# Issuing 18 of 24 output stores from GpSimd's queue in place of SyncE's

## The chip, the cores and the metric

The kernel runs on one core of one Trainium2 chip. The metric is the device time of one execution in microseconds; a kernel is given by the median of its runs. The engines are named as the profile names them: PE is TensorE (PEld its weight loads), DVE is VectorE, ACT is ScalarE, POOL is GpSimd, SP is SyncE. "SPq" and "POOLq" are the instruction streams of SyncE and GpSimd where they issue DMAs or wait.

## The reference

Inputs r, k, v, w, a, b have the shape (4 batches, 8 heads, 768 steps, 40), all float32. A recurrence runs over the steps; its output, laid out as 3072 tokens of 320, goes through a feed-forward block with a squared ReLU and 2048 hidden units. The output is float32, 3072 x 320.

```python
for t in range(S):
    y[:, :, t] = einsum('bhd,bhde->bhe', rt, state)
    Sa = einsum('bhde,bhe->bhd', state, at)
    state = state * wt[:, :, None, :] - einsum('bhd,bhe->bhde', Sa, bt) + einsum('bhd,bhe->bhde', vt, kt)
x = y.transpose(0, 2, 1, 3).reshape(3072, 320)
h = maximum(x @ w_in, 0.0)
out = (h * h) @ w_out
```

## The kernel before, in words

The 768 steps are cut into 6 chunks of 128. One chunk of one batch is a "load group" m (24 of them): six input tiles of 160 KB (NW, NK, NB, NA, NV, NR) are loaded for each by SyncE (`add_load`, line 272), into rings of four buffers per input. They are turned into the operands of the recurrence: ScalarE takes a logarithm of w (lnW, line 286) and exponentials (GI, GA); GpSimd or VectorE splits lnW in two differences (r at line 304, lo at line 308), multiplies k and b by GI (KB, line 331), and casts a, r and v (GA, RV, EVX, line 234). The operands are then transposed. For the later groups SyncE does that by a transposing DMA (line 374): KBT from KB, RVT from RV, A from GA. These DMAs stand in the same queue as the loads, and each waits until its source tile is written. For the earlier groups TensorE transposes through PSUM (line 346).

Each group has two "steps" of two head pairs, in which TensorE and VectorE work out the chunk's result within itself and with the state carried from the chunk before (matmuls at lines 477 to 590, products at lines 485, 571, 595). The result is YS. It leaves the head layout by four small DMAs on SyncE per feed-forward block (line 712, YS<-YS).

The feed-forward block (`add_ff`) runs over 14 sets of tokens (`FFS`): the groups 0 to 3 singly and then ten pairs. Each set makes hidden tiles: a product with WIN in a PSUM bank (line 723), a ReLU to hs on ScalarE or VectorE (line 731 or 733; a ring of three buffers), and a square to Gt on GpSimd, VectorE or ScalarE (line 742 or 740). For each group of the set the product of Gt with WOUT (line 760) is gathered in one bank, copied by ScalarE or VectorE to a tile osb of 128 x 320 float32 (a ring of three buffers) and stored to the output by one DMA of 160 KB (`store`, line 768). There are 24 such stores. The weights WIN and WOUT are loaded once, between 15 and 58 us, by DMAs that GpSimd issues (lines 680 and 688) and that cast to bfloat16 on the way.

The order in which the operations are emitted is written out by hand (`ORDER`), together with the choice of the engine for those that may run on more than one (`WAYS`). Each engine carries out its own instructions in the order in which they were emitted, so a store stands in its issuer's stream at the place that `ORDER` gives it, and what stands behind it on that engine waits for it. An osb buffer is written again only when the store of its former content has landed, by a semaphore. `add_guard` sums up energies of intermediate values; its verdict (`bad`, line 822) is read by all engines near the end and starts a general path if the fast one isn't accurate enough; with these inputs it is not taken.

TensorE's instructions are by name: line 477 `ca` (reads KBT and A's product AT), line 566 `ex` (reads RVT), line 509 corrections, line 582 `kbm`, line 590 `z`.

Of the kernel before, what the change touches and what calls it, by code (L numbers as in the profile page):

```python
# [18 lines left out]
def kernel(  # L19
# [12 lines left out]
    nc = tc.nc  # L32

    NB, NHH, T, D = r.shape
    L = 128
# [44 lines left out]
    def buf(ring, kind=None):  # L80
        b_ = Buf(ring, kind)
        if ring != "bank":
            row = rings.setdefault(ring, [])
            b_.n = len(row)
            row.append(b_)
        return b_

    def op(name, eng, rank, cost, lat, needs, bufs, fn, mode=None, alts=()):

        o = Op()  # L90
        o.name, o.eng, o.rank, o.cost, o.lat, o.mode = name, eng, rank, cost, lat, mode
        o.alts = [(eng, cost, lat), *alts] if alts else []
        o.needs, o.bufs, o.end, o.order = list(needs), list(bufs), None, len(ops)
        o.fn = (lambda: fn(o.eng)) if alts else fn
        o.dma = o.idle = None
        for b_ in o.bufs:
            b_.users.append(o)
        assert name not in ops, name
        ops[name] = o
# [21 lines left out]
    def act(n, more=0.0):  # L121
        return 0.093 + 0.00083 * n + more, 0.186 + 0.00083 * n

    def pe(n):
        return n, n + 0.165

    def vec(n, each=0.00104):
        return 0.065 + each * n, 0.148 + each * n
# [21 lines left out]
    for ring, shape in (("KB", [128, 2, NHH, 64]), ("GA", [128, 2, NHH, 64]),  # L150
# [9 lines left out]
        out=UTI[:], in_=ones_f[:], pattern=[[1, 128]],  # L160
# [5 lines left out]
        out=IDb[:], in_=ones_b[:], pattern=[[1, 128]],  # L166
# [3 lines left out]
    for s in range(2):  # L170
        nc.gpsimd.tensor_copy(out=IDs[64 * s:64 * s + D, :],
                              in_=IDb[64 * s:64 * s + D, 64 * s:64 * s + D])
    for i in range(26):
# [3 lines left out]
        out=UTb[:], in_=ones_b[:], pattern=[[1, 128]],  # L177
# [4 lines left out]
        out=MEX[:], in_=MEX[:], pattern=[[0, 4], [1, L]],  # L182
# [46 lines left out]
    def copy(eng, out, in_, scale=None):  # L229
        if eng == "ACT":  # L230
            nc.scalar.activation(out=out, in_=in_, func=ACTF.Copy,  # L231
                                 **({} if scale is None else {"scale": scale}))
        elif scale is None:
            (nc.gpsimd if eng == "POOL" else nc.vector).tensor_copy(out=out, in_=in_)
        else:
            nc.vector.tensor_scalar(out=out, in0=in_, scalar1=scale, scalar2=None, op0=ALU.mult)  # L236
# [22 lines left out]
    def sb(b_, shape, dtype):  # L259
        if b_.tile is None:  # L260
            pool = natp if b_.ring[0] == "N" else rot
            b_.tile = pool.tile(shape, dtype, name=b_.ring, tag=b_.ring,
                                bufs=RING[b_.ring if b_.ring in RING else "N"])
        return b_.tile
# [430 lines left out]
    FFS = [(0,), (1,), (2,), (3,)] + [(m, m + 1) for m in range(4, NBC, 2)]  # L695
    Gtb = [buf("Gt") for _ in FFS]

    def add_ff(h):
# [56 lines left out]
        for b_ in range(nb):  # L755
            opb, osbb = buf("bank", "ff"), buf("osb")

            def ff_out(part_, b_=b_, opb=opb):
                for j in range(part_ * NJ // 2, (part_ + 1) * NJ // 2):
                    nc.tensor.matmul(out=opb.tile[:, 0:DM], lhsT=Gtb[h].tile[:, j, b_, :],  # L760
                                     rhs=WOUT[:, j, :], start=(j == 0), stop=(j == NJ - 1))

            def copy_out(eng, opb=opb, osbb=osbb):
                copy(eng, sb(osbb, [128, DM], FP32)[:], opb.tile[:, 0:DM])

            def store(b_=b_, osbb=osbb):
                tok = (b0 + b_) * T + c * L
                nc.sync.dma_start(out=out[tok:tok + L, :], in_=osbb.tile[:])

            k = NJ // NU // 2  # L770
            for p in range(2):
                op(("op", h, b_, p), "PE", last + 12.8 + 1.8 * b_ + 0.3 * p, *pe(1.085),
                   [("Gt", h, k * p + i) for i in range(k)] + [("WOUT", 2 * p), ("WOUT", 2 * p + 1)]
                   + ([("op", h, b_, 0)] if p else []),
                   [Gtb[h], opb], lambda p=p, f=ff_out: f(p), "F")
            op(("osb", h, b_), "ACT", last + 13.5 + 1.8 * b_, *act(302), [("op", h, b_, 1)],
               [opb, osbb], copy_out, alts=[("DVE", *vec(320))])
            op(("st", h, b_), "SP", last + 1.6 + 1.8 * b_, 0.45, 0.45, [("osb", h, b_)], [osbb], store)
            ops["st", h, b_].dma = "h", 0.5
# [309 lines left out]
```

## Time and profile before

| | us |
|---|---|
| median of 3 runs | 272.27 |
| lowest and highest | 271.66 and 272.66 |
| the profiled execution | 272.03 |
| its span, first to last instruction | 270.3 |

The profiled execution ran at a mean granted TensorE clock of 0.981; the clock is below full only in the first quarter. DMA engines moved 37.61 MB, 34.33 MB of them through the queue of SyncE (75.6% of 16 engines' span) and 2.62 MB through that of GpSimd (6.6%).

How to read it: a row of a timeline has the start in us from the span's start, the duration in us, the engine, the source line, the operation, what it writes and reads, and how many were merged; in square brackets the idle time of the engine before it and what ended it. A row of the list of waits has who waited for whom, the total in us, the number of waits and the longest. A row of the stretches has, for each engine, its busy time and its instructions, and then the granted clock, the DMA engines' share and GB/s. A row of the DMA issues ends with the median time from issue to landing, in us. Matmuls are pipelined and overlap in the timeline, so TensorE's starts tell more than its durations.

### The profile page before, as it was taken

The page shows a single profiled execution, that of the slowest core. Times are in us where ns is not written, and L with a number is a line of the kernel's source. Part 1 is how long each engine was busy: PE and PEld are TensorE (multiplying, and loading weights), DVE is VectorE, ACT ScalarE, POOL GpSimd, SP SyncE. Part 2 cuts the span into 40 slices and gives each one's busy share as a digit, 9 for nine tenths or more (in the row PEclk, how much of TensorE's full clock was granted, in tenths as well). Part 3 has the DMA queues.
Part 4 walks back from the last instruction along what each step waited for, and adds up shares of the span by engine and source line. Part 5 has one row for each costly group of instructions (what it writes and reads, how often), then busy time and mean ns, then how long its engine had stood idle before and what let it go on. Part 6 is the DMA issues. An engine that isn't in the chain of part 4 may idle for free.

```text
span 270.3 us, 10143 instructions
## 1 busy us (share of the span) xinstructions
PE 254.8 (94%) x3944; PEld 205.7 (76%) x3944; DVE 241.0 (89%) x564; ACT 206.8 (77%) x542; POOL 186.2 (69%) x313
## 2 busy tenths in 40 slices
PE   7885989799999999999999999999999999999994
PEld 6653668578888778778888778888888777778773
DVE  7785899999999999999999999999999888898382
ACT  3474778888999979888999878787888767966560
POOL 4396947896979797799978668786945574143360
PEclk9998589999999999999999999999999999999999
DMA  7999999997983995898897889998999978904002
GB/s 120 172 179 158 155 168 174 166 183 124 158 150 59 184 150 94 157 182 145 162 175 143 149 156 150 184 140 160 165 124 118 180 130 166 153 11 112 6 29 75
DMA packets 184034, 37.61 MB, mean 139 GB/s; under 512 B 178544, under 2 KB 183664, under 8 KB 183984
## 3 DMA queue, kind: packets, MB, share of 16 engines
q1 hardware_dynamic: 181328, 34.33, 75.6%
q0 software_dynamic: 2656, 2.62, 6.6%
q8 instruction: 31, 0.51, 0.8%
q14 instruction: 19, 0.16, 0.2%
HBM read 28.84 MB, written 3.93 MB: 121 GB/s over the span
## 4 chain that ended last, share of the span: by engine, by line
PE 62%; DVE 14%; DMA 6%; SPq 5%; ACT 4%; issue 4%; POOL 3%; DVEq 0%; POOLq 0%; ACTq 0%
PE bank L723 19%; PE bank L760 14%; PE bank L346 5%; SPq L272 5%; PE bank L582 5%; PE bank L477 4%; DVE CN L485 4%; PE bank L509 3%; PE bank L566 3%; DVE EVX L571 3%; PE bank L300 2%; PE bank L590 2%; DMA KBT<-KB 2%; DVE YS L595 2%; DMA NA<-in_a_dram 2%
## 5 line engine op out<-in xcount | busy, mean ns | idle before, releaser
L723 PE MATMUL bank<-YS,WIN 120*128 120x256 bf16 (+3 forms) x672 | 75.0, 257 | 0.3 <-DVE CN L485 0.3
L571 DVE TENSOR_TENSOR EVX<-bank,MEX 128x512 bf16<-128x512 f32 x96 | 63.8, 679 | 2.2 <-PE bank L566 1.7
L485 DVE TENSOR_TENSOR CN<-bank,MCN 128x512 bf16<-128x512 f32 x96 | 62.8, 679 | 2.0 <-PE bank L477 1.3
L723 PEld LDWEIGHTS <-WIN 120*128 120x128 bf16 (+1 forms) x672 | 54.6, 97 | 7.6 <-issue 0.4
L760 PE MATMUL bank<-WOUT,Gt 128*128 128x320 bf16 x384 | 58.6, 299 | 0.0
L742 POOL TENSOR_TENSOR Gt<-hs 128x512 bf16<-128x512 bf16 x38 | 39.6, 1044 | 26.6 <-ACT hs L731 14.5
L731 ACT ACTIVATE hs<-bank 128x512 bf16<-128x512 f32 x74 | 42.9, 596 | 8.2 <-PE bank L723 3.2
L760 PEld LDWEIGHTS <-Gt 128*128 128x128 bf16 x384 | 34.9, 97 | 12.4 <-issue 0.2
L534 ACT ACTIVATE junk<-CN 128x512 bf16<-128x512 bf16 x48 | 30.1, 628 | 1.5 <-DVE CN L485 1.0
L526 POOL TENSOR_TENSOR x<-Mc,c 128x160 f32<-128x160 bf16 x41 | 20.8, 510 | 13.5 <-DVE c L522 11.8
L331 POOL TENSOR_TENSOR KB<-NB,GI 128x320 bf16<-128x320 f32 (+1 forms) x22 | 18.8, 856 | 12.7 <-DMA NB<-in_b_dram 12.6
L530 POOL TENSOR_TENSOR Cc<-x,EVX 128x160 bf16<-128x160 f32 x46 | 23.3, 513 | 2.9 <-DVE EVX L236 1.4
L509 PEld LDWEIGHTS <-CN 128*128 128x128 bf16 x384 | 19.6, 97 | 5.8 <-issue 1.8
L582 PE MATMUL bank<-EVX,KB 128*64 128x168 bf16 x384 | 23.4, 245 | 0.1
L331 POOL TENSOR_TENSOR KB<-NK,GI 128x320 bf16<-128x320 f32 (+1 forms) x23 | 19.7, 858 | 5.1 <-ACT GI L321 2.7
L740 ACT ACTIVATE Gt<-hs 128x512 bf16<-128x512 bf16 x35 | 21.7, 632 | 1.2 <-DVE hs L733 1.0
L231 ACT ACTIVATE TB<-bank 128x512 bf16<-128x512 bf16 (+1 forms) x29 | 16.8, 578 | 7.2 <-PE bank L552 4.4
L477 PE MATMUL bank<-AT,KBT 64*128 64x128 bf16 x384 | 19.8, 222 | 2.1 <-ACT KBT L231 1.2
L595 DVE TENSOR_TENSOR YS<-bank,GT 128x256 bf16<-128x256 f32 x48 | 19.6, 413 | 1.3 <-PE bank L582 0.8
L733 DVE TENSOR_SCALAR hs<-bank 128x512 bf16<-128x512 f32 x22 | 14.8, 684 | 5.9 <-issue 3.9
L599 DVE TENSOR_TENSOR UZ<-bank,GT 64x80 bf16<-64x80 f32 x80 | 18.5, 234 | 1.5 <-PE bank L590 0.5
L522 DVE TENSOR_TENSOR c<-bank,Mc 128x160 bf16<-128x160 f32 x48 | 14.9, 314 | 5.4 <-PE bank L509 5.0
(113 smaller groups left out, 587.6 us busy)
## 6 DMA issues: line engine op xcount, KB each, us to landing
NW<-in_w_dram SPq DMA_DIRECT2D x24, 160.0 KB
NB<-in_b_dram SPq DMA_DIRECT2D x24, 160.0 KB
NK<-in_k_dram SPq DMA_DIRECT2D x24, 160.0 KB
NA<-in_a_dram SPq DMA_DIRECT2D x24, 160.0 KB
NV<-in_v_dram SPq DMA_DIRECT2D x24, 160.0 KB
NR<-in_r_dram SPq DMA_DIRECT2D x24, 160.0 KB
out_dram<-osb SPq DMA_DIRECT2D x24, 160.0 KB
WOUT<-in_moe_w_out_dram POOLq DMA_DIRECT2D x4, 320.0 KB, 5.6
```

The costliest lines, as they stand in the source:

```text
L331: engine(eng).tensor_tensor(out=o.KB.tile[:, u, h, 0:D], in0=o.nat[key].tile[:, h], in1=o.GI.tile[:, h], op=ALU.mult)
L477: nc.tensor.matmul(out=quads(ca[s])[:, i, u, :], lhsT=o.KBT.tile[half(s), u, j0 + i, :], rhs=o.AT.tile[half(s), j0 + i, :], start=(i == 0 ...
L485: nc.vector.tensor_tensor(out=t_[:, :, s], in0=quads(ca[s]), in1=MCN[:], op=ALU.mult)
L509: nc.tensor.matmul(out=P[:, 2 * i + s], lhsT=CN[:, i, s, 1, :], rhs=X[:, 2 * i + s], start=False, stop=last, skip_group_check=True)
L534: nc.scalar.activation(out=t_, in_=CN_.tile[:, :, :, 1, :], func=ACTF.Square, accum_out=ACC[:, AN + st:AN + st + 1])
L571: nc.vector.tensor_tensor(out=EVX[:, :, s, 0:2 * LV].rearrange("p i (u x) -> p i u x", u=2)[:, :, :, 0:L], in0=quads(ex[s]), op=ALU.mult, ...
L582: nc.tensor.matmul(out=uy()[half(s), i, :], lhsT=o.KB.tile[:, u, 2 * (j0 + i) + s, :], rhs=EVX[:, i, s, LV * u:LV * u + LV], start=(i == 0 ...
L595: nc.vector.tensor_tensor(out=t_[:, p2, :], in0=uy()[:, :, 0:L], in1=o.GT.tile[:, j0:j0 + 2, 0:L], op=ALU.mult)
L723: nc.tensor.matmul(out=hp[:, u], lhsT=WIN[g][0:ROWS[g], j * 128:(j + 1) * 128], rhs=by_pair()[0:ROWS[g], g], start=(g == 0 and u == 0), st ...
L731: nc.scalar.activation(out=t_, in_=hpb.tile[:], func=ACTF.Relu)
L742: engine(eng).tensor_tensor(out=t_, in0=x_, in1=x_, op=ALU.mult)
L760: nc.tensor.matmul(out=opb.tile[:, 0:DM], lhsT=Gtb[h].tile[:, j, b_, :], rhs=WOUT[:, j, :], start=(j == 0), stop=(j == NJ - 1))
```

## The change

The stores of the sets 4 to 12 of 14 (`h` counts the sets), that is 18 of 24, are issued by GpSimd; those of the first four sets and of the last one stay with SyncE. A DMA issued by GpSimd goes through the other DMA queue. Every operation keeps its place in `ORDER`; in GpSimd's stream a store comes to stand between the operations that were emitted before and after it. The copies to osb, the buffers and the semaphore waits for data and buffers are the same.

```diff
             def store(b_=b_, osbb=osbb):
                 tok = (b0 + b_) * T + c * L
-                nc.sync.dma_start(out=out[tok:tok + L, :], in_=osbb.tile[:])
+                queue = nc.gpsimd if 4 <= h < len(FFS) - 1 else nc.sync
+                queue.dma_start(out=out[tok:tok + L, :], in_=osbb.tile[:])
```

## The prediction

> **What bounds the kernel now.** I read the engines' busy time first, then the same by stage, the chain that ended last, and TensorE's own two waits on it, because all 18 moved stores lie between 127 and 263 us.
>
> ```profile
> PE 254.8 (94%) x3944; PEld 205.7 (76%) x3944; DVE 241.0 (89%) x564; ACT 206.8 (77%) x542; POOL 186.2 (69%) x313
> ```
> ```profile
> core 0: us, PE busy (x) PEld busy (x) DVE busy (x) ACT busy (x) POOL busy (x), PEclk, DMA share, GB/s
> 127.00:200.00 73.00, 72.85 (x1160) 60.07 (x1159) 70.28 (x165) 62.46 (x176) 56.47 (x89) 1.00 0.97 156
> 200.00:235.00 35.00, 34.16 (x513) 27.42 (x512) 30.08 (x68) 27.21 (x68) 18.59 (x30) 1.00 0.87 146
> 235.00:262.00 27.00, 27.00 (x333) 21.87 (x331) 19.68 (x41) 17.16 (x40) 11.68 (x16) 1.00 0.21 51
> ```
> TensorE at full clock is the bound in every stretch that the change touches: of these 135 us it is idle 0.15 + 0.84 + 0 = 0.99 us. GpSimd is busy 56.47 + 18.59 + 11.68 = 86.74 us and idle 48.3. After 127 us SyncE, DMA and GpSimd stand in the chain in one stretch, 209 to 234 us:
>
> ```profile
> 209.18 3.60 DMA NB<-in_b_dram
> 212.92 0.85 POOL KB L331
> ...
> 214.45 1.01 POOL Gt L742
> 215.48 0.61 ACT hs L731
> ...
> 223.13 0.85 SPq L712
> 224.03 2.82 DMA NV<-in_v_dram
> ...
> 227.90 0.86 POOL KB L331
> 228.79 5.11 DMA KBT<-KB
> ```
> A load is issued by SyncE, lands, GpSimd works on it, and the next engine starts 0.02 to 0.03 us after GpSimd ends (214.45 + 1.01 to 215.48; 227.90 + 0.86 to 228.79). Here alone a microsecond of SyncE or of GpSimd reaches TensorE. It waits twice:
>
> ```profile
> 215.73 0.23 PE L477 MATMUL bank<-AT,KBT 64*128 64x128 bf16 x1
> 216.13 0.38 PE L477 MATMUL bank<-AT,KBT 64*128 64x128 bf16 x7 [0.17 <-ACT hs L731]
> ```
> ```profile
> 233.19 0.26 PE L509 MATMUL bank<-c,CN 128*128 128x40 bf16 x4
> 233.94 0.40 PE L477 MATMUL bank<-AT,KBT 64*128 64x128 bf16 x8 [0.50 <-DMA KBT<-KB]
> ```
> By starts, which do not hang on modelled ends, the first wait is 216.13 - 215.73 = 0.40 us less one matmul of under 0.05 (eight of this line take 0.40 with their latency), about 0.35. The second is 0.75 us less four matmuls of about 0.025, some 0.65.
>
> **The price of one moved store.** SyncE loses 18 issues; GpSimd gains 18. The output bytes, the copies into osb and the order on TensorE, VectorE and ScalarE stay.
>
> ```profile
> L768 SPq DMA_DIRECT2D out_dram<-osb x24: 333/524/881, 88.5 to 267.2; - x24
> ```
> ```profile
> 32.73 1.09 POOL L680 DMA_DIRECT2D WIN<-in_moe_w_in_dram  x2
> 40.88 0.81 POOL L688 DMA_DIRECT2D WOUT<-in_moe_w_out_dram  x1
> ```
> SyncE: 18 x 0.524 = 9.4 us of issue time go. GpSimd has issued no store yet; the nearest rows are a WIN load of 40 rows at 1.09 / 2 = 0.55 us and a WOUT load of 128 x 4 rows at 0.81. A store has 128 rows, so I take 0.55 + 0.26 x 88 / 472 = 0.60 us and keep 0.55 and 0.81 as ends. 18 x 0.60 = 10.8 us (9.9 to 14.6) fit four times into GpSimd's 48.3 idle us, so what counts is the place of each.
>
> **Where the new issues stand.** Numbered 1 to 24 in the order of SyncE, stores 5 to 22 move. In the built program each osb copy stands far enough ahead; the nearest is store 17, behind the x at 232.46:
>
> ```profile
> 230.25 0.43 ACT L231 ACTIVATE osb<-bank 128x320 f32<-128x320 f32 x1
> ```
> ```profile
> 232.46 0.60 POOL L526 TENSOR_TENSOR x<-Mc,c 128x160 f32<-128x160 bf16 x1 [2.86 <-DVE c L522]
> ```
> Its copy ends at 230.68, GpSimd comes at 233.06. Only 18 and 22 may find GpSimd waiting for the copy: 18 in the idle 6.59 us before 247.17 (below), 22 as its last operation. So no new wait for data holds GpSimd up. Most stores stand before a gap:
>
> ```profile
> 173.55 0.86 POOL L331 TENSOR_TENSOR KB<-NB,GI 128x320 bf16<-128x320 f32 x1
> 176.82 1.04 POOL L742 TENSOR_TENSOR Gt<-hs 128x512 bf16<-128x512 bf16 x1 [2.41 <-ACT hs L731]
> ...
> 221.27 0.49 POOL L526 TENSOR_TENSOR x<-Mc,c 128x160 f32<-128x160 bf16 x1 [1.44 <-DVE c L522]
> ...
> 247.17 1.04 POOL L742 TENSOR_TENSOR Gt<-hs 128x512 bf16<-128x512 bf16 x1 [6.59 <-DVE Gt L742]
> ...
> 262.20 1.04 POOL L742 TENSOR_TENSOR Gt<-hs 128x512 bf16<-128x512 bf16 x1 [0.35 <-DVE hs L733]
> ```
> ```profile
> 266.77 0.44 ACT L231 ACTIVATE osb<-bank 128x320 f32<-128x320 f32 x1 [4.01 <-PE bank L760]
> ```
> Stores 8 and 9 stand ahead of the Gt at 176.82: 1.2 us into 2.41 idle. Stores 13 and 14 come at 213.8 and 217.3; their 1.2 us end in the 1.44 idle before 221.27. Store 21 stands before 262.20: 0.60 - 0.35 = 0.25 us late at worst, for products that take TensorE some 4 us to the last copy at 266.77, so I take 0 (end: +0.25). If such a gap were gone, the next operation would be 0.60 us later.
>
> The one place with neither gap nor slack is store 13, between KB (212.92 to 213.77) and r. It moves r, Gt and so hs, which waits for Gt's buffer, by 0.60 us; TensorE starts at 216.13 right behind hs. **Cost: +0.60 us at 216** (0.55 to 0.81). Behind hs on ScalarE stand the osb copy at 218.12, after 2.05 idle us, and all that follows; the idle time covers them.
>
> **What SyncE gains.** 9.4 us only help where a load is late at TensorE, which leaves 216 and 234. For 216:
>
> ```profile
> 200.51 0.58 SPq L768 DMA_DIRECT2D out_dram<-osb  x1
> ...
> 204.85 1.43 SPq L374 DMA_TRANSPOSE A<-GA  x1
> ```
> ```profile
> 203.66 0.45 POOL L234 CAST GA<-NA 128x320 bf16<-128x320 f32 x1
> ```
> The store at 200.51, number 12, goes from SyncE, 0.58 less, but on GpSimd it stands before the cast to GA at 203.66, which now ends at 203.66 + 0.60 + 0.45 = 204.71. The transposing DMA waits for it and starts near 204.8 again, and NB at 209.18 stays. I take 0 (ends 0 and -0.35, that whole wait). For 234:
>
> ```profile
> 219.53 1.53 SPq L712 DMA_DIRECT2D YS<-YS  x2
> ...
> 222.53 0.54 SPq L768 DMA_DIRECT2D out_dram<-osb  x1
> ```
> ```profile
> 219.09 0.41 DVE L595 TENSOR_TENSOR YS<-bank,GT 128x256 bf16<-128x256 f32 x1
> ```
> At 219.53 SyncE waits for VectorE's YS, so all that it gained before is lost there. Behind it one store goes: NV, RV, KB and the transpose come 223.13 - 222.53 = 0.60 us earlier if YS is on time; if the 0.60 at 216 reaches YS, not at all. TensorE reaches this point 0.60 later by store 13, but was to wait 0.65: it starts between 233.90 (it is the late one) and 233.94 (the transpose is). So the wait swallows the cost: **-0.65 + 0.60 = -0.05, up to 0.** After 235 TensorE is busy without a gap.
>
> The sum: 0.60 at 216, -0.60 to -0.65 at 234, about 0 elsewhere: -0.05 us. On the profiled execution, whose 272.03 us are 270.3 of span and 1.7 around it, that is 272.0; this execution lies 0.24 below the median of the runs, so against 272.27 I forecast **272.2 us, no change.** Its own range, by a cost of 0.81 that is not swallowed and a wait of 0.65 that goes without cost, is 271.6 to 273.1.
>
> **Rivals.** *Faster by both waits (about 271.2).* SyncE runs ahead, GpSimd's store comes while NB is still on the way, and 0.35 + 0.65 = 1.0 us go. For it: at 212.92 GpSimd starts right behind the landing of NB. Against it: the program's order has store 13 after KB. TensorE's 0.99 us of idle time allow no more, some tenths hidden by modelled ends apart.
>
> *Slower, by late landing (about 274.3).* There are three osb buffers, so a copy waits until the store three before has landed. Store 8 is issued by GpSimd after 173.55 + 0.86 = 174.41, and its buffer is written again at 177.71:
>
> ```profile
> 177.71 0.44 ACT L231 ACTIVATE osb<-bank 128x320 f32<-128x320 f32 x1
> ...
> 218.12 0.44 ACT L231 ACTIVATE osb<-bank 128x320 f32<-128x320 f32 x1 [2.05 <-PE bank L760]
> ```
> ```profile
> 179.00 1.49 PE L723 MATMUL bank<-YS,WIN 120*128 120x256 bf16 x12
> ```
> ```profile
> WOUT<-in_moe_w_out_dram POOLq DMA_DIRECT2D x4, 320.0 KB, 5.6
> WIN<-in_moe_w_in_dram POOLq DMA_DIRECT2D x6, 160.0 KB, 4.4
> ```
> 3.30 us are allowed. GpSimd's loads land after 4.4 and 5.6 us; a store of 160 KB without their cast may land sooner. At 5.6 ScalarE stands 2.3 us at 177.71; the bank is read next by the matmul at 179.00, 0.85 after the copy's end, so TensorE loses 2.3 - 0.85 = 1.45. Store 13, issued at 213.77, must have landed by 218.12: 5.6 is 1.25 late there, less the 0.60 by which store 13 has moved that copy itself: 0.65. 1.45 + 0.65 = 2.1 us, 274.3. It decides from a landing of 3.30 + 0.85 = 4.15 us on; at 4.4 it costs 0.25.
>
> The Trainium skill speaks for this one: its page "SBUF — State Buffer", section "SBUF: two separate sides", says that a DMA issued from GpSimd starves for descriptors while VectorE holds their shared port in a two-port mode, and gives some 620 ns alone against some 3100 beside such a copy. With 2.5 us more on 4.4, an estimate by that page, a store would land after 6.9 and the sum would be about 276.9. The trace does not show a stretched issue (0.55 and 0.81 us in the rows above), and of the landing only the medians below; I give this 0.03 of that rival's chance.
>
> *Slower, not given back (about 273.2).* Stores 11 and 12 too stand before work that transposing DMAs wait for, a store at 0.81 outruns the 1.44 idle us at 221 and makes Gt late there, and the 0.60 to 0.81 at 216 pass YS and delay the transpose of 228.79 as well. Then +0.81 and 0.1 to 0.2 from the others: 1.0 us. Against it: in the list of waits the one at 234 is TensorE's only one on such a transpose.
>
> ```profile
> PE bank L477 <- DMA KBT<-KB: 0.5, 1, 0.5
> ```
>
> *Nothing freed.* SyncE spends the 9.4 us in waiting for load buffers; that is part of the forecast.
>
> **Numbers.** Forecast 0.45, faster by both waits 0.15, late landing 0.22, not given back 0.18. 0.5% of 272.27 is 1.36 us, about what a measurement tells from no change. The forecast lies within it; of the faster case 0.06 are beyond (TensorE's idle time is nearly all used up by then); of late landing 0.21, of not given back 0.13. So faster 0.06, same 0.60, slower 0.34. The range reaches from the faster case, 271.2, to just above late landing, 274.4.
>
> **What would show it.** Right: GpSimd's stores take 0.55 to 0.81 us; its Gt near 214.4 is 0.6 later, TensorE's wait near 216 about 0.95 and that near 234 under 0.1; the osb copies wait for nothing but TensorE. Wrong: an idle stretch of ScalarE ahead of an osb copy that a DMA of the output ends (late landing); both waits gone (faster); TensorE idle for over 2 us between 127 and 262; or a store on GpSimd of well over 0.81 us.

## The result, and the profile after

| | us |
|---|---|
| before, 5 runs | 272.66 (271.66 to 276.05) |
| after, 5 runs | 276.12 (273.97 to 277.34) |
| ratio | 1.0128, 95% interval 1.0081 to 1.0175 |
| the profiled execution after, its span | 276.70, 275.0 |

The kernel is slower by 1.3%, outside the predicted range. The execution time of this kernel spreads by over 1% from run to run, so that a ratio is known to 0.4 or 0.5%, some 1.0 to 1.5 us; therefore most of what follows is read from traces. Two of the twelve profiles below, of the second and the sixth run, fell in disturbed executions of 274.88 and 277.59 us; only the ends of these two and rows that the others repeat are used.

The engines' busy time after, and the same three stretches as before:

```profile
PE 253.5 (92%) x3944; PEld 204.9 (75%) x3944; DVE 240.2 (87%) x564; ACT 206.7 (75%) x542; POOL 196.6 (72%) x331
```
```profile
127.00:200.00 73.00, 72.86 (x1160) 60.08 (x1159) 69.98 (x164) 62.38 (x176) 60.59 (x96) 1.00 0.94 158
200.00:235.00 35.00, 33.53 (x497) 26.96 (x495) 30.13 (x69) 27.67 (x69) 22.40 (x36) 1.00 0.89 138
235.00:262.00 27.00, 26.52 (x337) 21.36 (x338) 18.42 (x39) 16.12 (x38) 11.90 (x18) 1.00 0.24 55
```

TensorE was idle 0.99 us in these 135 us before; it is idle 0.14 + 1.47 + 0.48 = 2.09 us now. That is 1.1 us, but the span has grown by 4.7. GpSimd's instructions grew by the 18 stores. They cost what was forecast, 0.57 us each, and land after 3.0 us (the groups of instructions, and the DMA issues):

```profile
L769 POOL DMA_DIRECT2D out_dram<-osb x18 | 10.3, 571 | 1.4 <-ACT osb L231 1.4
```
```profile
out_dram<-osb POOLq DMA_DIRECT2D x18, 160.0 KB, 3.0
```

Most of the 4.7 us lies where TensorE has finished. These rows are the last stores and the last copy, from the timeline of the changed kernel:

```profile
265.12 0.57 POOL L769 DMA_DIRECT2D out_dram<-osb  x1
...
267.80 0.49 DVE L234 COPY osb<-bank 128x320 f32<-128x320 f32 x1 [0.86 <-DMA out_dram<-osb]
268.32 0.97 SPq L769 DMA_DIRECT2D out_dram<-osb  x2
268.47 0.44 ACT L231 ACTIVATE osb<-bank 128x320 f32<-128x320 f32 x1 [4.01 <-PE bank L760]
```

Before, the last copy ran from 266.77 for 0.44 us and the span ended at 270.3: a tail of 3.1 us from the end of the last copy to the end. Now it ends at 268.91 and the span at 275.0: 6.1 us. So the tail holds 3.0 of the 4.7 us and the body, up to the last copy, 1.7. The views of the profile do not count what fills the tail, since register, branch and semaphore instructions are not busy time there; the trace's records do. The DMAs that GpSimd issues are called software DMAs below, and the two long records INC_SWDGE_SEM and DRAIN behind the branch are called their closing, by their names and by what the runs show of them. GpSimd's last records, start and duration in us:

```
before                                      after
265.63 0.05 COMPARE_BRANCH (on bad)         267.53 0.06 COMPARE_BRANCH (on bad)
266.13 0.02 EVENT_SEMAPHORE                 270.30 0.02 EVENT_SEMAPHORE
266.45 0.48 INC_SWDGE_SEM                   270.63 0.83 INC_SWDGE_SEM
266.96 1.21 DRAIN                           271.49 2.68 DRAIN
269.54 0.02 EVENT_SEMAPHORE (all engines)   274.21 0.02 EVENT_SEMAPHORE (all engines)
```

Before, GpSimd had closed its software DMAs at 268.17, and what all waited for was the landing of the last store at 269.0. Now GpSimd stands 2.72 us behind the branch that skips the general path (0.44 before), then closes for 1.8 us longer (0.83 + 2.68 against 0.48 + 1.21), and all engines wait for it: the last store lands at 270.84, the drain ends at 274.17.

Of the body's 1.7 us, 0.70 are there at 66 us, before any store is moved; the same shift was between -1.15 and +1.87 us in the twelve experiments and is chance. Measured from there, TensorE's starts come 0.51 us sooner between 217 and 230 us, 0.71 later from 236 on, and 1.00 later from 257 on. The rows of the two places are in the chain of waits of the changed kernel:

```profile
216.37 0.33 PE bank L477 x8
...
223.72 3.74 DMA NV<-in_v_dram
...
228.49 0.86 POOL KB L331
229.37 5.94 DMA KBT<-KB
235.35 0.40 PE bank L477 x8
```
```profile
252.44 0.77 DVE YS L595 x2
...
254.95 0.65 SPq L712
255.60 0.04 issue
255.64 2.52 DMA YS<-YS
258.16 0.05 issue
258.21 1.39 PE bank L723 x11
```

At 216 no wait stands ahead of TensorE. At 235 it waits for KBT as before, but 1.72 us in place of 0.50, and the transposing DMA takes 5.94 in place of 5.11 us. At 258 it waits for a YS DMA; in the profile before it had 0.46 us to spare there.

### The profile page after: what moved, and what is told of

The parts are those of the page before. It is cut to its first block, busy times and chain, and to the rows that moved or that the text cites. A ratio compares the mean times of both kernels' runs of the same rounds, so it can differ in the third digit from the quotient of the medians.

```text
span 275.0 us, 10138 instructions
## 1 busy us (share of the span) xinstructions
PE 253.5 (92%) x3944; PEld 204.9 (75%) x3944; DVE 240.2 (87%) x564; ACT 206.7 (75%) x542; POOL 196.6 (72%) x331
## 4 chain that ended last, share of the span: by engine, by line
PE 66%; DVE 14%; DMA 6%; POOL 4%; issue 4%; ACT 3%; SPq 1%; DVEq 0%; POOLq 0%; ACTq 0%
PE bank L723 20%; PE bank L760 14%; PE bank L346 6%; PE bank L582 5%; PE bank L477 5%; PE bank L509 3%; DVE CN L485 3%; PE bank L566 3%; DVE EVX L571 3%; PE bank L300 2%; DMA KBT<-KB 2%; PE bank L590 2%; DVE YS L595 2%; POOL KB L331 2%; PE bank L546 2%
## 5 line engine op out<-in xcount | busy, mean ns | idle before, releaser
L331 POOL TENSOR_TENSOR KB<-NB,GI 128x320 bf16<-128x320 f32 (+1 forms) x22 | 19.5, 886 | 12.1 <-DMA NB<-in_b_dram 5.6
```

Of the source, the lines that this page charges most:

```text
L331: engine(eng).tensor_tensor(out=o.KB.tile[:, u, h, 0:D], in0=o.nat[key].tile[:, h], in1=o.GI.tile[:, h], op=ALU.mult)
```

## The experiments

In all of them "stand" is the time from the end of the branch on `bad` to the next record of that engine, "tail" the time from the end of the last osb copy to the end of the span, and a branch has a number by its place among the records of its engine. How long a DMA takes is from its issue to the last count on its semaphore; where no chain shows it, it is from the trace's records. The stores are numbered as in the prediction. Where an expectation counts software DMAs (10 in the kernel before, 28 in the changed one), four more belong to it: the trace has 14 issues by GpSimd before, ten for WIN and four for WOUT, and so 32 after.

### Is it the branch or the closing of the software DMAs? (runs 1 to 4)

Runs 1 and 2 are the kernels before and after without these lines; the general path is left out, the fast path is whole:

```diff
-    with tc.If(flag > 0):
-        general()
```

> The kernel before without the general path (the branch on `bad` and all behind it left out; the fast path is whole). Control for the next run. Branch theory (what was lost at the end of the changed kernel is the time that SyncE and GpSimd stand behind that branch: 2.02 and 2.72 us there, 0.14 and 0.44 before): the kernel before loses nothing there, so this one is the same within 0.5 us, 272.3 +- 0.5. Drain theory (it is GpSimd's closing of its software DMAs, 2.68 us against 1.21): the same here, as its 1.21 us are over before the last store lands.

Measured: 272.39 us, ratio 0.9972 (0.9928 to 1.0016), tail 3.12 us.

> The changed kernel without the general path, nothing else. From the end of the last osb copy to the end of the span it took 6.09 us with the general path, 3.09 before. Branch theory: the stand of 2.72 us behind the branch goes, GpSimd's closing begins about 2.3 us sooner, and the tail is 3.5 to 4.0 us; the time is 1.7 (body) + 0.5 to 0.9 above that of the run without the general path before. Drain theory: the closing is as long as before, the tail stays at 5.5 to 6 us, the time 4 to 4.7 above the control.

Measured: ratio 0.9977 (0.9921 to 1.0032), tail 2.80 us, and the drain is 2.68 us as in the changed kernel. Without the branch the whole loss cannot be seen any more. The drain is as long as with the branch, but it starts sooner, at 268.46, while the last stores are not yet issued, and it ends at 271.14, before the last of them lands at 272.16, so that it is hidden. The tail came out shorter than either theory said. The time came out lower too: the 1.7 us for the body held 0.7 of chance, and the remaining 1.0 us lies within the interval.

Runs 3 and 4 move only some of the stores:

```diff
-                queue = nc.gpsimd if 4 <= h < len(FFS) - 1 else nc.sync
+                queue = nc.gpsimd if 4 <= h < 9 else nc.sync                 # run 3
+                queue = nc.gpsimd if 9 <= h < len(FFS) - 1 else nc.sync      # run 4
```

> Only the stores of sets 4 to 8 (10 of them, the last near 190 us) on GpSimd, the other 14 on SyncE. If the closing drain depends on how many software DMAs were issued: it takes between 1.21 (10 of them) and 2.68 us (28), at 20 of them about 2.0 us. If it depends on how late the last one is: 1.2 us. Body theory (the longer wait for the transposing DMA at 234, +1.0, comes from stores issued after 196 us): TensorE's wait at 234 is again 0.6, and the time is within 0.7 of the kernel before if the branch stall is gone too, 2 us above it if the branch stalls as in the changed kernel.

Measured: ratio 0.9984 (0.9935 to 1.0033). Drain 2.02 us; GpSimd stands 0.44 us, tail 3.2 us.

> Only the stores of sets 9 to 12 (8 of them, from near 200 us on) on GpSimd. By number of software DMAs (18) the closing drain takes about 1.9 us, by the lateness of the last one 2.7 us as in the changed kernel. Body theory: the wait at 234 is as in the changed kernel, 1.7 us; if instead the earlier stores made the transposing DMA late, 0.6 us. Branch theory: what SyncE and GpSimd stand behind the branch depends on how many instructions they have issued, so it may be neither 0.4 nor 2.7 us; drain theory: it is as in the changed kernel, as the last software DMA is at the same place.

Measured: ratio 1.0175 (1.0086 to 1.0265), from two executions only (273.05 and 276.27 us). Drain 1.86 us; GpSimd stands 2.52 us and SyncE 1.63, tail 4.9 us.

The drain follows the count of software DMAs to a hundredth: 1.21 us for 14, 1.86 for 22, 2.02 for 24, 2.68 for 32, which is 0.07 + 0.0814 us each. The stand is there in run 4 and not in run 3. Two things could make that difference: that the stores of run 4 are late, or that its branch is number 428 in GpSimd's stream and that of run 3 number 426. The expected 1.7 us at 234 in run 4 was a miss: its KBT took 4.2 us and TensorE did not wait.

### Late stores, or the place of the branch? (runs 5 to 8)

Run 5 moves only set 12:

```diff
-                queue = nc.gpsimd if 4 <= h < len(FFS) - 1 else nc.sync
+                queue = nc.gpsimd if h == len(FFS) - 2 else nc.sync
```

Run 6 moves no store and adds empty instructions:

```diff
                 nc.sync.dma_start(out=out[tok:tok + L, :], in_=osbb.tile[:])
+                if h == 6 and b_ == 0:
+                    for _ in range(20):
+                        nc.gpsimd.nop(hint="keep", nofuse=True)
```

> Only stores 21 and 22 (set 12), the last of the moved ones, on GpSimd: 12 software DMAs, the last as late as in the changed kernel. In the four kernels so far the branch on `bad` is GpSimd's instruction 417 (before), 426 (early), 428 (late), 437 (changed), and it then stands 0.44, 0.44, 2.52, 2.72 us; SyncE's is 343, 331, 328, 316, and it stands 0.14, 0.48, 1.63, 2.02. Here they are 421 and 339. Place theory (the stand is the fetch of the instructions behind the jump and depends on where in the stream the branch lies): no stand, under 0.5 us on both, tail of 3.1 us from the last copy to the end. Lateness theory (the stand comes from software DMAs issued shortly before the end): GpSimd stands 2.5 us. Closing drain by the count of software DMAs, 0.40 + 0.0814 us each: 1.37 us.

> The kernel before, no store moved, with 20 empty instructions in GpSimd's stream (at store 9) and none elsewhere: its branch is number 437, as in the changed kernel; SyncE's stays 343. Place theory: GpSimd stands 2.5 to 2.7 us behind the branch though no store is moved, SyncE 0.14; GpSimd's closing (INC 0.48, drain 1.21) then ends near 270.1 in place of 268.2, and the tail grows by about 0.5 us. Lateness theory: 0.44 us, tail 3.1.

Run 7 is the changed kernel with the second half of `general`, from `IDf` on, cut out (a path not taken here) and, beside each moved store:

```diff
+                if queue is nc.gpsimd:
+                    for _ in range(2):
+                        nc.sync.nop(hint="keep", nofuse=True)
```

> The changed kernel, all 18 stores on GpSimd, with a shorter way for the jump: the second half of the general path (never taken here) is left out, so that GpSimd jumps from 437 to 493 and not to 568, and two empty instructions per moved store on SyncE put its branch at 352. Place theory: both stand under 0.5 us; the tail is about 3.7 us (GpSimd: 0.5 + 0.4 + 0.83 + drain 2.68, ends near the landing of the last store), 2.4 less than the changed kernel; time 273 to 274. Lateness theory: GpSimd stands 2.7 us, the tail stays at 6.1, time 276. Body: TensorE's wait at 234 for the transposing DMA was 1.7 and 1.1 us in the two profiles with all 18 stores moved and 0 to 0.5 in the four others; if it comes from the moved stores it is over 1 us again.

Run 8 is the changed kernel unaltered.

> The changed kernel once more. Place theory: the stand behind the branch is 2.7 (GpSimd) and 2.0 us (SyncE) again, the tail 6.1 us, the closing drain 2.68. If the stand were chance, it would be another. Body: if the longer wait at 234 comes from the moved stores, it is over 1 us again; if it is the spread from run to run of that transposing DMA (3.2 to 5.9 us so far), it may be anything from 0 to 1.9.

A target is the number in GpSimd's stream at which the jump ends: 131 records behind the branch, the length of the general path there, or 56 in run 7.

| kernel | GpSimd's branch, target | GpSimd stands | SyncE stands | drain | tail |
|---|---|---|---|---|---|
| before | 417, 548 | 0.44 | 0.14 | 1.21 | 3.1 |
| 5, last two | 421, 552 | 0.43 | 0.14 | 1.37 | 2.8 |
| 3, early | 426, 557 | 0.44 | 0.48 | 2.02 | 3.2 |
| 4, late | 428, 559 | 2.52 | 1.63 | 1.86 | 4.9 |
| 6, before with 20 nops | 437, 568 | 2.76 | 1.53 | 1.22 | 4.1 |
| after | 437, 568 | 2.72 | 2.02 | 2.68 | 6.1 |
| 8, after again | 437, 568 | 2.65 | 1.95 | 2.68 | 6.0 |
| 7, after, shorter jump | 437, 493 | 0.43 | 0.14 | 2.68 | 3.8 |

Run 5 gave 270.17 and 276.81 us, too few executions for a ratio; run 6 273.86, ratio 0.9980 (0.9938 to 1.0022). The tail of run 6 is 1.0 us longer, where 0.5 was expected; that alone would be a ratio of 1.0037, above the interval. So run 6 shows the stand in its one profile, and its time does not bear it out; the reason is open.

The place decides. Run 6 has the stand with no store moved; run 5 moves the last stores and has none; run 7 has all 18 stores and none, as its jump ends nearer. All targets up to 557 come without a stand, all from 559 on with one of 2.1 to 2.3 us more; in runs 9 to 12 below (targets 491 and 550) GpSimd stands 0.43 or 0.44 us. SyncE's number has nothing to do with it, and there run 6 was a miss: SyncE stood 1.53 us with the number it had before. In the records SyncE goes on at 271.41, 268.77 and 273.62 us in the changed kernel and runs 4 and 6, each time within 0.1 us of the end of GpSimd's INC_SWDGE_SEM, which points to a wait for GpSimd. The 0.48 us of SyncE in run 3 are not of this kind (GpSimd's INC_SWDGE_SEM had ended 1.03 us earlier) and stay open.

In time: runs 7 and 8, on one chip, gave 274.70 and 276.72 us, ratios 1.0041 (1.0003 to 1.0078) and 1.0090 (1.0046 to 1.0134). The 2.0 us between the medians, 1.3 by the ratios, agree within the noise with the 2.2 us by which their tails differ. So with the stand gone the changed kernel is some 1.1 us slower than before and no longer 2.5.

Is the stand a fetch of instructions? The trace has rows for such fetches, of which the changed kernel has one more (the list of DMA queues, before and then after: transfers, MB, share):

```profile
q14 instruction: 19, 0.16, 0.2%
```
```profile
q14 instruction: 20, 0.16, 0.2%
```

The packets of this queue say more. The four profiles with a stand have 20 fetches of 8 KB each within the span, the eight others with the branch 19. In all twelve a fetch starts 0.93 to 1.18 us behind the end of GpSimd's branch. Without a stand GpSimd has gone on by then; with one it stands through this fetch and goes on 1.15 to 1.27 us after its end. So the stand has a fetch in it each time; that the fetch is what ends it was not tried by itself.

The Trainium skill, page "Runtime: NRT & Kernel Launch", section "Instruction fetch mechanics", says that a taken branch whose target is outside the current two-page window makes the engine wait for a DMA of the target page. The jump with a stand from a certain target on, and the fetch in each stand, agree with that; the fetches here are of 8 KB each, 0.16 MB / 20, not the 16 KB that the page gives.

### What costs TensorE 1 us? (runs 9 to 12)

The four profiles with all 18 stores on GpSimd (after, 2, 7, 8) have a KBT at 234 of 5.80 to 5.94 us, the others up to here 3.2 to 5.1. One thing in which they differ from most of the others is store 16, which GpSimd issues just behind the start of that DMA. The timeline before and after:

```profile
228.11 0.51 SPq L768 DMA_DIRECT2D out_dram<-osb  x1
228.79 1.25 SPq L374 DMA_TRANSPOSE KBT<-KB  x1
...
233.94 0.40 PE L477 MATMUL bank<-AT,KBT 64*128 64x128 bf16 x8 [0.50 <-DMA KBT<-KB]
```
```profile
229.37 1.23 SPq L374 DMA_TRANSPOSE KBT<-KB  x1
229.74 0.57 POOL L769 DMA_DIRECT2D out_dram<-osb  x1
...
235.35 0.40 PE L477 MATMUL bank<-AT,KBT 64*128 64x128 bf16 x8 [1.72 <-DMA KBT<-KB]
```

Before, the store stood ahead of the transpose in one queue and had landed at 230.12. Now both are under way together, and land together at 235.30 and 235.31. Run 9 is run 7 with two stores back on SyncE; run 10 is the kernel before with the same two alone on GpSimd:

```diff
-                queue = nc.gpsimd if 4 <= h < len(FFS) - 1 else nc.sync
+                queue = (nc.gpsimd if 4 <= h < len(FFS) - 1
+                         and (h, b_) not in [(9, 1), (11, 1)] else nc.sync)            # run 9
+                queue = nc.gpsimd if (h, b_) in [(9, 1), (11, 1)] else nc.sync         # run 10
```

> The kernel of the seventh run (changed kernel, shorter way for the jump) with two of the 18 stores back on SyncE: number 16, which GpSimd issues 0.37 us after SyncE has begun to issue the transposing DMA that TensorE awaits at 234, and number 20, issued 0.1 us after the last YS DMA that TensorE awaits at 256. Collision theory: these two stores, by the side of the awaited transfers and no longer behind or ahead of them in one queue, lengthen them (KBT 5.8 to 5.9 us in four profiles with all 18 moved, 3.2 to 5.1 in the six others; last YS 2.4 to 2.5 against 1.78). With them back: last YS 1.78 us and no wait of TensorE at 256 (0.28 less), KBT at most 5.1 us and a wait at 234 of at most 0.6 us; from 60 us to the end TensorE loses 0 to 0.4 us against the kernel before, where the seventh run lost 1.1; time about 273.7. Rival (the loss at 234 is from SyncE's and GpSimd's other order, KB later by the stores ahead of it): KBT 5.8 again, wait 1.2, only the 0.28 at 256 goes.

> The kernel before with those two stores alone (16 and 20) on GpSimd; branch of GpSimd is number 419, so no stand there. Collision theory: last YS 2.4 to 2.5 us and 0.28 us of wait at 256; KBT 5.5 to 5.9 us and a wait of 1.0 to 1.4 us at 234; TensorE 0.9 to 1.1 us later at the end than the kernel before from 60 us on. Rival: 256 as told, but KBT at most 5.1 and the wait at 234 as before or less (0 to 0.7), since the run with only the late stores moved had both store 16 beside KBT and a KBT of 4.2 us.

(9, 1) is store 16, but (11, 1) turned out to be number 19 and not 20, so these runs say nothing on 256. On 234 they are clear; the timelines of run 9 and of run 10:

```profile
228.91 0.52 SPq L769 DMA_DIRECT2D out_dram<-osb  x1
229.62 1.24 SPq L374 DMA_TRANSPOSE KBT<-KB  x1
...
234.23 0.40 PE L477 MATMUL bank<-AT,KBT 64*128 64x128 bf16 x8
```
```profile
229.85 1.23 SPq L374 DMA_TRANSPOSE KBT<-KB  x1
230.20 0.60 POOL L769 DMA_DIRECT2D out_dram<-osb  x1
...
235.69 0.40 PE L477 MATMUL bank<-AT,KBT 64*128 64x128 bf16 x8 [1.42 <-DMA KBT<-KB]
```

With store 16 back, KBT takes 3.26 us and TensorE does not wait; with it alone beside the transpose KBT takes 5.80 us and TensorE waits 1.42. By time both are within 0.3% of the kernel before (1.0028, 0.9983 to 1.0072; 1.0006, 0.9960 to 1.0052); the 0.8 us that TensorE is late in run 10 is 0.3% too, so that the times neither show it nor speak against it.

Run 11 is run 7 with 16 and 20 back; run 12 is the kernel before with 13 and 20 alone on GpSimd:

```diff
-                queue = nc.gpsimd if 4 <= h < len(FFS) - 1 else nc.sync
+                queue = (nc.gpsimd if 4 <= h < len(FFS) - 1
+                         and (h, b_) not in [(9, 1), (10, 1)] else nc.sync)            # run 11
+                queue = nc.gpsimd if (h, b_) in [(8, 0), (10, 1)] else nc.sync         # run 12
```

> In the ninth run the second store put back was number 19, not 20. Here it is 16 and 20; else as there (shorter way for the jump, 16 stores on GpSimd). Collision theory: last YS at 256 1.78 us with 0.46 us to spare for TensorE, KBT at most 5.1 us, no wait at 234 over 0.6; from 60 us to the end TensorE loses nothing against the kernel before (-0.6 to +0.2 us); the tail is 3.6 us (26 software DMAs, closing drain 2.51 us), 0.5 longer than before; time equal to the kernel before within 0.5%, at most 0.5 us above it. Rival (the moved stores cost elsewhere too): TensorE 0.5 us or more later at the end.

Measured: 272.29 us, ratio 1.0000 (0.9964 to 1.0036), tail 3.61, drain 2.51, last YS 1.78 us, KBT 3.27 us, no wait at 234 or 256. With 16 of the 24 stores on GpSimd, and SyncE spared as many issues, the kernel is as fast as before and no faster.

> The kernel before with stores 13 and 20 alone on GpSimd. Store 13 is the term that the prediction put at +0.60 us: issued between KB and r, it should move r, Gt and hs by 0.60 and TensorE's start at 216 with them (wait of about 0.95 by starts, +0.6 against the kernel before), given back at 234 where the wait of 0.65 goes. Rival: NB lands sooner as SyncE has one store less ahead of it, KB starts sooner, and the wait at 216 is as before or less. Store 20 alone: if it stands beside the last YS DMA that takes 2.4 to 2.5 us in place of 1.78 and TensorE waits 0.2 to 0.3 us at 256.

Measured: 272.89 us, ratio 1.0005 (0.9960 to 1.0050). The last YS takes 2.50 us with store 20 issued 0.08 us behind it, and TensorE comes 0.30 us later there: confirmed. For store 13 the run decides little, as TensorE was already 0.5 us late at 200 us, before any moved store; at 216 it lost 0.2 more and at 234 gave 0.1 back. Run 3 and run 11, which both have store 13 on GpSimd and 16 on SyncE, show it better.

TensorE's starts against the profile before, each less the same difference at 64 to 70 us (us):

| kernel | 211 to 215 | 217 to 230 | 236 to 250 | 257 to 262 |
|---|---|---|---|---|
| after | -0.13 | -0.51 | +0.71 | +1.00 |
| 8, after again | -0.12 | +0.14 | +0.87 | +1.16 |
| 7, after, shorter jump | -0.15 | +0.26 | +0.94 | +1.12 |
| 1, before, no general path | +0.52 | +0.38 | -0.14 | -0.14 |
| 3, early | -0.05 | +0.74 | +0.17 | +0.17 |
| 4, late | +0.20 | -0.04 | -0.61 | -0.31 |
| 5, last two | +0.43 | +0.15 | -0.40 | -0.40 |
| 9, 16 and 19 back | +0.40 | +0.27 | -0.29 | -0.12 |
| 10, 16 and 19 alone | +0.17 | -0.13 | +0.80 | +0.79 |
| 11, 16 and 20 back | -0.13 | +0.52 | -0.05 | -0.05 |
| 12, 13 and 20 alone | +0.72 | +0.91 | +0.82 | +1.12 |

Run 4 stays open: there too store 16 went beside the transpose, 0.45 us behind its start, and KBT took only 4.2 us. So with store 16 beside it that DMA took 5.80 to 5.94 us in five profiles of six; what spared the sixth was not tried. Without that store it took 3.2 to 5.1 us in eight profiles, and the cause of this spread is open as well.

## Why the prediction was wrong, step by step

- **The price of a store: right.** 0.571 us against 0.60, within 0.55 to 0.81.
- **Store 13 at 216: right as a mechanism, and given back as forecast where store 16 is not in the way; in the changed kernel its 0.60 was too much, as NB's landing moved too.** In run 3, KB, store, r and Gt stand in a chain, and hs waits for it:

```profile
213.61 0.57 POOL out_dram L769
214.20 0.73 POOL r L304
214.93 1.00 POOL Gt L742
215.96 0.61 ACT hs L731
216.60 0.38 PE bank L477 x7
```

TensorE waited 0.97 us there (0.95 was forecast), came 0.79 us later, and lost the wait at 234, 0.57 us; in run 11 it was 0.65 later and 0.57 back. In the profile of the changed kernel the 0.60 did not come: KB began at 212.48, though TensorE ran 0.57 us later than before. It still began 0.13 us behind NB's landing, as in every profile, and the store still stood behind it; but NB landed 1.00 us sooner against TensorE. So "NB at 209.18 stays", with a gain of 0, did not hold against TensorE, and SyncE ran ahead as the rival "faster by both waits" said. In runs 7 and 8 NB landed 0.18 and 0.32 sooner and the cost was 0.41 and 0.26, which is 0.60 less this gain to 0.02.

- **"-0.60 to -0.65 at 234": failed.** TensorE came 0.68 to 1.22 us later there in the three profiles of the table with all 18 stores, not 0.6 sooner. The working had taken the DMA's 5.11 us as given and asked only when it would be issued. Store 16 was costed as an issue on GpSimd; that its 160 KB would no longer lie ahead of the transpose but beside it was not looked at. Nor was the transpose issued 0.60 sooner: less the shift at 64 to 70 us it went 0.12 us sooner in the profile of the changed kernel, and 0.18 and 0.06 later in runs 7 and 8. In the first NV, issued sooner, took 3.74 in place of 2.82 us, and GpSimd casts it ahead of KB. In the other two NV landed 0.27 and 0.46 sooner, but KB began 0.16 and 0.17 us behind the landing of NB, whose issue took 1.32 and 1.39 us. These rows of SyncE, before and after, show that issue:

```profile
224.59 0.71 SPq L272 DMA_DIRECT2D NB<-in_b_dram  x1
```
```profile
224.27 1.35 SPq L272 DMA_DIRECT2D NB<-in_b_dram  x1
```

- **"After 235 TensorE is busy without a gap": failed by 0.2 to 0.3 us.** Store 20, which SyncE issued at 246.53, reaches the head of GpSimd's stream at 255.75, next to the last YS DMA; that takes 2.52 in place of 1.78 us, 0.74 more against 0.46 to spare (YS landed at 256.05 before). TensorE before, then the store and TensorE after:

```profile
256.51 2.71 PE L723 MATMUL bank<-YS,WIN 120*128 120x256 bf16 x23
```
```profile
255.75 0.57 POOL L769 DMA_DIRECT2D out_dram<-osb  x1
...
258.21 1.06 PE L723 MATMUL bank<-YS,WIN 120*128 120x256 bf16 x8
```

The Trainium skill, page "DMA: Bandwidth & Descriptors", section "SWDGE vs HWDGE vs iDMA", says that the two kinds of DMA feed different queues inside each DMA engine and that the engine takes turns between them. Both collisions agree with it; the trace does not show the turns themselves.

- **"About 0 elsewhere": the step that failed most, by 3.0 us.** The sum ended with the last store. What GpSimd does after its last store has no row in the views that were read, and was taken as unchanged. It was not, in two ways: 2.3 us for the stand, because the stores and their waits lengthen GpSimd's stream by 20 records and push the jump's target past a limit between 557 and 559, and about 0.7 us (run 7's tail of 3.8 less 3.1) for a closing that grows by 18 x 0.0814 = 1.47 us of drain and 0.35 of INC_SWDGE_SEM, most of it hidden behind the last landing.
- **The rivals.** "Late landing", priced at 274.3, is nearest in number and wrong in kind: no copy on ScalarE waits for an output DMA, and the one on VectorE that does, 0.86 us at 267.80, ends before the last copy starts. The starved issue of the Trainium skill's page "SBUF — State Buffer", section "SBUF: two separate sides", is not seen: 0.57 us for the issue and a landing of 3.0 us. "Not given back" has nearly the size of the loss at 234, but not its way: the transpose was issued at most 0.18 us later and took longer. Of the signs of being wrong, TensorE idle for over 2 us came true with 2.09. "Nothing freed" was right: run 11 has 16 stores off SyncE, its collisions and the stand gone, and is equal to before.

The causes add to 2.3 + 0.7 + 1.0 to 1.2 = 4.0 to 4.2 us. The two ratios of the changed kernel give 3.5 us (2.2 to 4.8) and 2.5 us (1.3 to 3.7): the sum lies in the first interval and above the second, so that the terms of single traces are somewhat large as a mean. That the stand and the two collisions are the causes does not hang on it: the stand was put in by itself (run 6) and taken away (run 7), store 16 put in and taken back (runs 10 and 9, with 19 beside it), and store 20 too (runs 12 and 11, with 13 and 16 beside it). Each rests on traces, mostly one profile a kernel; only the stand shows in the times as well (runs 7 and 8), and for store 16 run 4 remains an exception.

## What to carry to other kernels

A sum for a moved DMA needs three more rows than its issue: what its bytes will now lie beside (look for the awaited transfer that starts within its landing time), where it comes up in the new engine's stream, and what that engine does after its last instruction, down to the end of the span. An issue taken off a queue is worth nothing while that queue waits for data anyway. Where code that is jumped over follows the kernel, compare the records behind the branch before putting a change of a few instructions down to what it does.

## What the runs showed of the hardware

- GpSimd's closing drain takes 0.07 us and 0.0814 us more for each software DMA of the program, wherever it was issued (1.21, 1.37, 1.86, 2.02, 2.51 and 2.68 us for 14, 16, 22, 24, 30 and 32).
- Behind a taken branch GpSimd goes on after 0.44 us, or after 2.5 to 2.8 us where the target lies from a certain place on (none up to 557, all from 559); in one profile 20 empty instructions made the difference.
- A small YS DMA on SyncE's queue, 1.77 to 1.81 us long alone, took 2.3 to 2.5 us in all seven profiles in which GpSimd issued a store of 160 KB 0.05 to 0.11 us behind it. The YS DMA issued 0.8 us ahead of the same store took 1.76 to 1.86, as ever.
